# Where the FFN's moving operands begin in SBUF: one offset instead of fourteen

## The chip, the core and the metric

The kernel runs on one core of a Trainium2 chip. The metric is the device time of one execution in microseconds (us). TensorE (PE in the profile) multiplies matrices, VectorE (DVE), ScalarE (ACT) and GpSimd (POOL) work element by element, and SyncE (SP) issues the transfers. SBUF is the working memory: 128 partitions, each a run of bytes, in which every buffer has one byte address for all partitions. PSUM receives the results of the matrix multiplications.

A matmul has two operands in SBUF. The **stationary** operand, the weights, is loaded by an instruction of its own (LDWEIGHTS, engine PEld in the profile). The **moving** operand is then streamed past it, one column after another; a column is four bytes in each partition here. This text is about the byte address at which the moving operand begins, and speaks of it modulo 512 bytes: its *offset*.

## What is computed

```python
def _attn_ref(x, w_r, w_i, b_r, b_i):            # x: (8, 3008, 256)
    X = np.fft.rfft(x, axis=1)
    Yr = Xr @ w_r - Xi @ w_i + b_r
    Yi = Xr @ w_i + Xi @ w_r + b_i
    Yr = np.sign(Yr) * np.maximum(np.abs(Yr) - lam, 0.0)   # the same for Yi
    return np.fft.irfft(Yr + 1j * Yi, n=x.shape[1], axis=1)

def _moe_ref(x, w_in, w_out):                     # x: (24064, 256)
    h = x @ w_in                                  # (24064, 2048)
    g = h - np.tanh(h)
    return g @ w_out                              # (24064, 256)
```

The result of the first function, flattened to 24064 rows, is the input of the second, which the text calls the FFN.

## The kernel before

**The spectral part.** A sequence of 3008 is transformed as 64 times 47. Per batch, `Forward` does the transform over 47, `Spectrum` the one over 64, the linear layer, the shrinking and one half of the way back, and `Chunk.time` the other half. Between them the data goes through DRAM. This is a small share of the matmuls.

**The FFN.** Its 24064 rows are cut into 52 chunks: 50 of 470 columns (five groups of 94) and two of 282. A chunk goes through 16 steps, one for each 128 of the 2048 hidden columns, so there are 832 steps. A step has two halves:

- `up` (the matmuls of line 428): six matmuls into the PSUM buffer `h`. ScalarE then takes tanh (line 431), VectorE subtracts (line 433).
- `down` (line 449): six matmuls that add to the chunk's two results `o`, and that are finished at the 16th step.

Values are kept in two parts each, a rounded one and its remainder (`_h` and `_l`: `yh`, `yl` for the FFN's input, `gh`, `gl` for the hidden values, `win_h`, `win_l`, `wout_h`, `wout_l` for the weights), and three of the four products are made: hence six matmuls with 2 x 3 pairs. In `up` the moving operand is, in this order, `yh` part 0, `yh` part 1, `yh` part 0, `yh` part 1, `yl` part 0, `yl` part 1. In `down` it is `gh`, `gh`, `gl`, and again `gh`, `gh`, `gl`. With 470 columns there are 800 steps and so 9600 such matmuls; the other 384 have 282.

**The order of the work.** It is written out by hand. The main loop runs `up` two steps ahead of `down` (`AHEAD = 2`), and puts pieces of the spectral part between them from a table of slots. No scheduler moves anything.

**The buffers.** `yh` and `yl` have two buffers each, one for even and one for odd chunks; a buffer holds two parts of `PITCH` columns, of which 470 are used. `gh` and `gl` have three buffers each, used in turn, step after step. `PITCH` is 520, so the next part or buffer begins 2080 bytes further on. A pool places its buffers one behind the other, and the pools lie one behind the other in the order in which they are opened. `below`, a small constant for the shrinking of the first batch, lies in the first pool behind the FFN's weights; nearly everything else is behind it.

As the program is built, the FFN's weights begin at 128 modulo 512, and so does each slice of 128 columns of them, since such slices are 512 bytes long. The moving operands lie as follows:

| moving operand | offset of its buffers |
|---|---|
| `yh` part 0, part 1, even chunks | 256, 288 |
| `yl` part 0, part 1, even chunks | 384, 416 |
| `yh` part 0, part 1, odd chunks | 320, 352 |
| `yl` part 0, part 1, odd chunks | 448, 480 |
| `gh`, three buffers | 0, 32, 64 |
| `gl`, the buffers that go with them | 128, 160, 96 |

Of the kernel before, what the change touches and what calls it, by code (L numbers as in the profile page):

```python
# [10 lines left out]
F32 = mybir.dt.float32  # L11
# [55 lines left out]
def spectral_ffn(ctx, tc, x, w_r, w_i, b_r, b_i, w_in, w_out, f1, f2, i1, i2, out):  # L67
    nc = tc.nc
    P = 128
# [2 lines left out]
    CP = 5  # L72
    CT = CP * 94
    NF = FF // P
    PITCH = 520
    PSUM = bass.MemoryType.PSUM

    const = ctx.enter_context(tc.tile_pool(name="const", bufs=1))
# [314 lines left out]
    class Chunk:  # L393
# [14 lines left out]
        def time(self, t):  # L408
            n = self.n
            if t == 0:  # L410
                self.yh = work.tile([P, 2, PITCH], F32R, name="yh", tag="yh")
                self.yl = work.tile([P, 2, PITCH], F32R, name="yl", tag="yl")
            ps = ps_f.tile([P, 512], F32, name="ps_i2", tag="f")
# [8 lines left out]
        def up(self, f):  # L422
# [10 lines left out]
            nc.vector.tensor_tensor(out=g[:, :n], in0=h[:, :n], in1=th[:, :n], op=ALU.subtract)  # L433
            gh = ffn.tile([P, PITCH], F32R, name="gh", tag="g_h")
            nc.scalar.copy(out=gh[:, :n], in_=g[:, :n])  # L435
            gl = ffn.tile([P, PITCH], F32R, name="gl", tag="g_l")
            nc.vector.tensor_tensor(out=gl[:, :n], in0=g[:, :n], in1=gh[:, :n].bitcast(F32), op=ALU.subtract)  # L437
# [58 lines left out]
    with tc.manual_schedule(engines={E.PE, E.Activation, E.DVE, E.Pool, E.SP}):  # L496
# [6 lines left out]
        def keep_warm(n):  # L503
            for _ in range(n):
                nc.tensor.matmul(idle, warm[:, :P], warm, start=True, stop=True)

        keep_warm(8)
        below = const.tile([P, 32], F32, name="below")
        nc.vector.memset(below, -LAM)
        f1f = load_whole(f1, [P, P], "f1")  # L510
        first = [Forward(0, ch) for ch in range(NP // XC)]
# [169 lines left out]
```

## Time and profile before

| | us |
|---|---|
| time, median of 3 runs | 2746.91 (2746.25 to 2747.99) |
| time of the profiled execution | 2745.83 |
| its span, first to last instruction | 2744.1 |
| PE busy in it | 2707.5 |
| PEld busy | 2386.7 |
| VectorE busy | 1742.6 |
| ScalarE busy | 1375.6 |

In the profile, L428 is line 428 of the listing. A group's row gives its number of instructions, then busy us and the mean duration of one in ns, then the idle time of its engine just before them, with what ended it. The duration of a matmul there reaches past the start of the next one, because matmuls are pipelined: what a matmul costs is the time from its start to the start of the next one, and this text calls that its *interval*. The view by windows gives, for stretches that the reader chooses, each engine's busy time and its number of instructions; its last row is the sum over all stretches asked for, and the mean of one.

### The profile page before, as it was taken

Reading aid. Unit: us, or ns where it says so; the run is one execution under the profiler, and the core shown is the slowest. Engines: PE = TensorE matmul, PEld = TensorE weight load, DVE = VectorE, ACT = ScalarE, POOL = GpSimd, SP = SyncE. Lnnn points to the kernel's source line nnn. Section 1 sums busy time; section 2 is a strip of 40 time slices with the busy share of each in tenths; the row PEclk is TensorE's granted clock in tenths of the full one; section 3 lists DMA queues with packets and bytes.
Section 4 is the critical chain, followed back from the end, with each engine's and each line's share of the span. In section 5 each row is a group of like instructions: output and inputs, shape, how many; then the busy total and the mean of one; then the engine's idle time right before and its main releaser. Section 6 shows DMA issues by size and latency. Waiting matters only on the chain.

```text
span 2744.1 us, 36889 instructions
## 1 busy us (share of the span) xinstructions
PE 2707.5 (99%) x14114; PEld 2386.7 (87%) x14114; DVE 1742.6 (64%) x3059; ACT 1375.6 (50%) x2571; POOL 58.2 (2%) x47
## 2 busy tenths in 40 slices
PE   8799999999999999999999999999999999999999
PEld 5578888998889998898988998888988998888889
DVE  5796776667556666567655666656665666655555
ACT  3564455544554455545455444645455444444444
POOL 2130000000000000000000000000000000000000
PEclk9999999999999999999999999999999999999999
DMA  7432113111131113211023110311103111000000
GB/s 213 151 103 66 45 63 112 42 49 36 42 108 49 38 39 99 67 45 50 27 64 94 41 50 30 114 52 51 39 28 116 49 38 40 35 22 22 20 18 17
DMA packets 105217, 163.52 MB, mean 60 GB/s; under 512 B 7440, under 2 KB 71056, under 8 KB 104944
## 3 DMA queue, kind: packets, MB, share of 16 engines
q1 hardware_dynamic: 105040, 161.16, 18.8%
q8 instruction: 111, 1.82, 0.3%
q14 instruction: 66, 0.54, 0.1%
HBM read 86.16 MB, written 74.97 MB: 59 GB/s over the span
## 4 chain that ended last, share of the span: by engine, by line
PE 93%; DVE 4%; DMA 1%; ACT 1%; issue 1%; POOL 0%; SPq 0%; DVEq 0%; ACTq 0%; POOLq 0%
PE o L449 37%; PE h L428 37%; PE ps_v L297 4%; PE ps_i L415 4%; PE ps_f L277 3%; PE ps_t L297 2%; PE ps_f L225 1%; PE ps_f L227 1%; PE ps_f L226 1%; DVE y L322 1%; PE ps_i L332 1%; PE ps_i L333 1%; PE ps_i L334 1%; DMA a<-st 0%; DVE gl L437 0%
## 5 line engine op out<-in xcount | busy, mean ns | idle before, releaser
L433 DVE TENSOR_TENSOR g<-h,th 128x470 f32<-128x470 f32 (+1 forms) x832 | 531.9, 639 | 580.3 <-ACT th L431 576.8
L431 ACT ACTIVATE th<-h 128x470 f32<-128x470 f32 (+1 forms) x832 | 464.0, 558 | 792.4 <-PE h L428 791.1
L437 DVE TENSOR_TENSOR gl<-g,gh 128x470 fp32r<-128x470 f32 (+1 forms) x832 | 532.8, 640 | 289.3 <-ACT gh L435 220.5
L435 ACT CAST gh<-g 128x470 fp32r<-128x470 f32 (+1 forms) x832 | 484.1, 582 | 390.9 <-DVE g L433 380.9
L449 PE MATMUL o<-gh,wout_l 128*128 128x470 f32 (+1 forms) x1664 | 634.9, 382 | 1.2 <-ACT gh L435 1.2
L449 PE MATMUL o<-gl,wout_h 128*128 128x470 f32 (+1 forms) x1664 | 620.8, 373 | 3.4 <-DVE gl L437 3.3
L449 PE MATMUL o<-gh,wout_h 128*128 128x470 f32 (+1 forms) x1664 | 621.6, 374 | 0.0
L428 PE MATMUL h<-yh,win_l 128*128 128x470 f32 (+1 forms) x1664 | 487.8, 373 | 5.2 <-DVE g L433 4.7
L428 PE MATMUL h<-yh,win_h 128*128 128x470 f32 (+1 forms) x1664 | 485.6, 372 | 0.0
L428 PE MATMUL h<-yl,win_h 128*128 128x470 f32 (+1 forms) x1664 | 483.9, 372 | 0.0
L428 PEld LDWEIGHTS h<-yh,win_l 128*128 128x128 f32 x1664 | 312.2, 189 | 50.2 <-DVE g L433 6.6
L449 PEld LDWEIGHTS o<-gl,wout_h 128*128 128x128 f32 x1664 | 313.3, 188 | 47.8 <-DVE gl L437 7.1
L428 PEld LDWEIGHTS h<-yh,win_h 128*128 128x128 f32 x1664 | 310.8, 188 | 42.2
L449 PEld LDWEIGHTS o<-gh,wout_l 128*128 128x128 f32 x1664 | 313.7, 189 | 38.6 <-issue 1.6
L428 PEld LDWEIGHTS h<-yl,win_h 128*128 128x128 f32 x1664 | 311.6, 188 | 41.0
L449 PEld LDWEIGHTS o<-gh,wout_h 128*128 128x128 f32 x1664 | 313.7, 189 | 33.7
L322 DVE TENSOR_TENSOR y<-tb,ps_v 64x256 f32<-64x256 f32 x384 | 160.1, 417 | 10.5 <-ACT tb L369 6.5
L415 PEld LDWEIGHTS ps_i<-i,zin 96*128 96x128 f32 x1024 | 128.4, 194 | 5.0 <-issue 1.8
L415 PE MATMUL ps_i<-i,zin 96*128 96x94 f32 x1024 | 130.0, 275 | 1.1 <-DMA zin<-z 1.1
L277 PEld LDWEIGHTS ps_f<-f,at 128*128 128x128 f32 x768 | 101.2, 192 | 14.3 <-issue 9.0
L277 PE MATMUL ps_f<-f,at 128*128 128x128 f32 x768 | 102.9, 276 | 6.4 <-DMA at<-a 6.4
L92 DVE TENSOR_TENSOR x_l<-xt,x_h 94x512 fp32r<-94x512 f32 x112 | 78.6, 708 | 45.1 <-ACT x_h L91 45.1
(99 smaller groups left out, 2098.4 us busy)
## 6 DMA issues: line engine op xcount, KB each, us to landing
xt<-in_x SPq DMA_DIRECT2D x64, 384.0 KB, 3.7
at<-a SPq DMA_DIRECT2D x96, 256.0 KB, 2.8
z<-zo SPq DMA_DIRECT2D x96, 256.0 KB, 2.3
out<-ot SPq DMA_DIRECT2D x50, 470.0 KB, 3.0
a<-st SPq DMA_DIRECT2D x56, 384.0 KB, 3.1
zin<-z SPq DMA_DIRECT2D x42, 480.0 KB, 4.1
w_raw<-in_moe_w_in SPq DMA_DIRECT2D x8, 512.0 KB, 4.1
w_raw<-in_moe_w_out SPq DMA_DIRECT2D x8, 512.0 KB, 4.1
```

The lines of the kernel that those rows point to most:

```text
L92: rest.tensor_tensor(out=lo, in0=src, in1=hi.bitcast(F32), op=ALU.subtract)
L225: nc.tensor.matmul(pv, f1h, xl, start=True, stop=False)
L277: nc.tensor.matmul(pv[:, t, jj], self.at[:, jj, t * P:(t + 1) * P], rhs, start=True, stop=True)
L297: nc.tensor.matmul(dst, lhs[:, t], rhs[:, t, :], start=n == 0, stop=n == 5)
L322: nc.vector.tensor_tensor(out=y[ri * 64:(ri + 1) * 64, jj, :], in0=common(jj, ri), in1=self.vv[jj * 64:(jj + 1) * 64, ri * D:(ri + 1) * D] ...
L415: nc.tensor.matmul(ps[:, k * 94:(k + 1) * 94], self.zt[:, k, t * P:(t + 1) * P], i2t[:, p * 94:(p + 1) * 94], start=True, stop=True,)
L428: nc.tensor.matmul(h[:, :n], lhs[:, t, f * P:(f + 1) * P], rhs[:, t, :n], start=k == 0, stop=k == 5)
L431: nc.scalar.activation(out=th[:, :n], in_=h[:, :n], func=AF.Tanh)
L433: nc.vector.tensor_tensor(out=g[:, :n], in0=h[:, :n], in1=th[:, :n], op=ALU.subtract)
L435: nc.scalar.copy(out=gh[:, :n], in_=g[:, :n])
L437: nc.vector.tensor_tensor(out=gl[:, :n], in0=g[:, :n], in1=gh[:, :n].bitcast(F32), op=ALU.subtract)
L449: nc.tensor.matmul(self.o[t][:, :n], lhs[:, f, t * P:(t + 1) * P], rhs[:, :n], start=f == 0 and k == 0, stop=f == NF - 1 and k == 2,)
```

## The change

```diff
-    PITCH = 520
+    PITCH = 512
...
-        below = const.tile([P, 32], F32, name="below")
+        below = const.tile([P, P + 8], F32, name="below")
         nc.vector.memset(below, -LAM)
```

`PITCH` falls to 512 columns, so parts and buffers are 2048 bytes apart, and an offset no longer changes from one to the next. `below` grows from 32 to 136 columns, 416 bytes, which shifts what lies behind it. As the program is built, all fourteen moving operands of the table above now begin at 160 modulo 512. The weights of the FFN lie ahead of `below` and stay at 128. Most of the other buffers (`xt`, `zin`, `at`, the linear layer's weights, the temporary ones) go from 256 or 0 to 160 as well.

No instruction is added, removed or moved on any engine. The one row that differs is VectorE's, right at the start of the program, where it fills a constant of zeros, makes the tile `warm` of it, and fills `below`:

```order
 L498 MEMSET zero 128x512
 L500 CAST warm<-zero 128x512
-L509 MEMSET below 128x32
+L509 MEMSET below 128x136
 L241 COPY st<-ps_f_133 96x512
 L241 COPY st<-ps_f_143 96x512
```

The fill keeps its place and gets 104 more columns.

## The prediction

> **What bounds the kernel.** I read the page's busy times first, then the chain that ended last, then the groups of the two FFN lines with shapes kept apart, and then the waits of PE.
>
> ```profile
> PE 2707.5 (99%) x14114; PEld 2386.7 (87%) x14114; DVE 1742.6 (64%) x3059; ACT 1375.6 (50%) x2571; POOL 58.2 (2%) x47
> PE 93%; DVE 4%; DMA 1%; ACT 1%; issue 1%; POOL 0%; SPq 0%; DVEq 0%; ACTq 0%; POOLq 0%
> L449 PE MATMUL o<-gh,wout_l 128*128 128x470 f32 x1600 | 615.8, 385 | 1.2 <-ACT gh L435 1.2
> L449 PE MATMUL o<-gl,wout_h 128*128 128x470 f32 x1600 | 602.0, 376 | 3.4 <-DVE gl L437 3.3
> L428 PE MATMUL h<-yh,win_l 128*128 128x470 f32 x1600 | 474.2, 377 | 5.2 <-DVE g L433 4.7 <-ACT yh L419 0.3
> PE h L428 <- DVE g L433: 4.7, 4, 1.9
> PE o L449 <- DVE gl L437: 3.3, 7, 0.7
> ```
>
> PE is busy 99% of the span and is 93% of the chain. In the FFN it hardly waits: 4.7 and 3.3 us in all, in 4 and 7 cases, for the two operands that VectorE makes. So the time is the sum of the intervals of PE's matmuls, and the question is what one of the 9600 intervals of 470 columns is worth before and after. VectorE and ScalarE, at 64% and 50%, have room; whatever the new addresses do to them is behind PE.
>
> The mean duration in the group rows mixes all buffers and reaches over the next start, so I cut PE's time into halves of a step. Here is a stretch with nothing but FFN matmuls, in windows from one half's first matmul to the next half's first: `up`, `down` from the buffers at 0/128, `up`, `down` at 64/96, `up`, `down` at 32/160 (`gh`/`gl`). The columns are the window, its length, the busy time of PE, PEld, DVE, ACT and POOL with the number of their instructions, PE's granted clock, the DMA share and GB/s.
>
> ```profile
> 2375.54:2376.83 1.29, 1.29 (x8) 1.12 (x7) 0.68 (x2) 0.00 (x0) 0.00 (x0) 1.00 0.70 209
> 2376.83:2378.11 1.28, 1.28 (x8) 1.13 (x6) 0.43 (x1) 0.56 (x1) 0.00 (x0) 1.00 0.49 167
> 2378.11:2379.39 1.28, 1.28 (x8) 1.13 (x7) 0.63 (x2) 0.59 (x1) 0.00 (x0) 1.00 0.00 0
> 2379.39:2380.66 1.27, 1.27 (x8) 1.13 (x7) 0.66 (x2) 0.56 (x1) 0.00 (x0) 1.00 0.00 0
> 2380.66:2381.93 1.27, 1.27 (x7) 1.12 (x6) 0.62 (x2) 0.59 (x1) 0.00 (x0) 1.00 0.00 0
> 2381.93:2383.24 1.31, 1.31 (x7) 1.14 (x6) 0.71 (x2) 0.56 (x1) 0.00 (x0) 1.00 0.00 0
> ```
>
> Each window holds six matmuls (the counts include neighbours that reach in). PE has no idle time in any, the granted clock is 1.00 in all, and still six equal matmuls take 1.27 us in one and 1.31 in another. The buffers differ, and the spread, 3%, is many times what this measurement can tell from no change, about 0.2% or 5.5 us.
>
> **What an offset is worth.** I took all halves of this kind that run without a foreign matmul and without a stop (no interval of 240 ns or more), in one window each, and read the sum row; the first 190 of each kind, or all where there are fewer. In order: `down` at 0/128 (190), `down` at 32/160 (190), `down` at 64/96 (190), `up` of even chunks, 256 to 416 (138), `up` of odd chunks, 320 to 480 (144).
>
> ```profile
> sum 245.27, PE 245.27; mean PE 1.29
> sum 244.69, PE 244.69; mean PE 1.29
> sum 243.08, PE 243.08; mean PE 1.28
> sum 176.40, PE 176.40; mean PE 1.28
> sum 184.61, PE 184.61; mean PE 1.28
> ```
>
> Divided by six times the count, a mean interval is 215.2, 214.6 and 213.2 ns in `down`, and 213.0 and 213.7 in `up`. The three buffers are used equally, and so are the two chunk parities: the mean of `down` is 214.3, of `up` 213.4, of both **213.85 ns**.
>
> The trace has no matmul at 160 that follows one at 160, so the new interval must be taken from neighbours. I sorted single intervals by the offset of their own operand and of the next one, 190 windows each. In order: 32 then 32; 64 then 64; 0 then 0; 32 then 160; 160 then 32; 384 then 416; 0 then 128.
>
> ```profile
> sum 40.88, PE 40.88; mean PE 0.22
> sum 40.48, PE 40.48; mean PE 0.21
> sum 40.55, PE 40.55; mean PE 0.21
> sum 40.75, PE 40.75; mean PE 0.21
> sum 40.66, PE 40.66; mean PE 0.21
> sum 39.86, PE 39.86; mean PE 0.21
> sum 41.26, PE 41.26; mean PE 0.22
> ```
>
> That is 215.2, 213.1, 213.4, 214.5, 214.0, 209.8 and 217.2 ns. Three things are to be seen. The order of two offsets matters, up to 7 ns. Two equal offsets are nothing special: from 213.1 to 215.2. And of the equal ones, the pair at 32 is the slow one; 160 is 32 plus 128, and both lie 32 past a multiple of 64, while 0 and 64 do not.
>
> At this point a rule speaks against any effect. The Trainium skill, page "SBUF — State Buffer", section "Who interferes with whom", says that PE has two independent read ports, one for the moving operand and one for the weights, and never waits on anyone; the page "TensorE: Matmul & The Clock Gate", section "Back-to-back issue gap", gives N/2.4 + 2.5 ns, by which an estimate for 470 columns is 198.3 ns wherever the operand lies. By these the change is worth nothing. The rows above disagree twice: the mean is 213.85 ns, and buffers differ.
>
> **The change part by part.**
>
> *The FFN's operands, 9600 matmuls of 470 columns.* The nearest rows are those of the only buffers that hold an operand at 160, `down` at 32/160: 214.6 ns. There all six operands lie 32 past a multiple of 64, as all will after the change. Against 213.85 that is 0.79 ns more (from the unrounded 214.64), and 9600 x 0.79 = **+7.6 us**. Nearby bounds: the mean of 32-then-160 and 160-then-32, 214.2, gives +3.7 us; 32-then-32, 215.2, gives +12.6. Far bounds: 64-then-64 gives -7.7 us, 384-then-416 gives -39, 0-then-128 gives +32. I take the nearest row, and keep the far ones for the range.
>
> *The 384 matmuls of 282 columns.* At the same 0.79 ns they are 0.3 us.
>
> *The spectral part.* Its matmuls with large moving operands go from 256 to 160. The rows of three of its lines show their size:
>
> ```profile
> L297 PE MATMUL ps_v<-w_h,xh 128*128 128x256 f32 x336 | 67.6, 283 | 0.0
> L226 PE MATMUL ps_f<-x_h,f_l 94*96 94x512 f32 x112 | 44.7, 399 | 0.0
> L334 PE MATMUL ps_i<-z_h,i_h 128*128 128x512 f32 x84 | 33.1, 394 | 0.0
> ```
>
> Line 297 has 1512 such matmuls in six groups, lines 225 to 227 and 332 to 334 have 588. At most 283, 399 and 394 ns each, these are under 0.7 ms. No row shows them at another offset; if they move as the FFN's do, by 0 to 0.5% (+0.4% in the nearest row), it is 0 to 3 us, and as far below nothing by the pair at 64. These durations reach over the next start, so the true share is smaller; I take +1.
>
> *The fill of `below`.* It grows by 104 columns.
>
> ```profile
> 0.92 0.48 DVE L498 MEMSET zero<- 128x512 f32 x1 [0.92 <-PEq L660]
> 1.93 0.09 DVE L509 MEMSET below<- 128x32 f32 x1
> 7.43 0.69 DVE L241 COPY st<-ps_f 96x512 f32<-96x512 f32 x1 [5.42 <-PE ps_f L219]
> ```
>
> A fill of 512 columns takes 0.48 us and one of 32 takes 0.09, so 104 more are 104/480 of the 0.39 between them: 0.08 us. VectorE is then idle for 5.42 us, which covers it; without the cover it costs 0.08.
>
> *The element-wise work.* VectorE's and ScalarE's operands move as well. Should they get slower, the share of PE's waits above (8 us in all) is what they reach now, and they would have to fill the rest of their idle time before PE sees it. I count nothing.
>
> The sum is 7.6 + 0.3 + 1 = +8.9 us, on a profiled execution of 2745.8 us: 2754.7. That execution is 1.1 us below the median, so the forecast for the median is 2755.8, rounded to **2756 us**.
>
> **The rivals.**
>
> *No effect.* The offset only sorts the intervals by chance, because another thing that goes with the buffer sets them: the position in the half, or the weights. For it: 0-then-0 and 64-then-64 are within 0.8 ns of the mean. Against it: `down` has the same six positions and, over the steps, the same weights for each of its three buffers, and these differ by 1.9 ns. It gives 2747, and with the spectral part up to 3 us either way. The rules of the Trainium skill quoted above lead to this case.
>
> *Equal operands settle, and it becomes faster.* At the start, `keep_warm` (line 505) runs 18 matmuls of 512 columns with the same moving operand and the same weights. The windows hold its intervals 2 to 10 and the last 7:
>
> ```profile
> 21.32:23.41 2.09, 2.09 (x10) 1.69 (x9) 1.60 (x3) 0.00 (x0) 0.86 (x1) 1.00 0.72 176
> 23.41:25.00 1.59, 1.59 (x8) 1.31 (x7) 1.34 (x2) 0.44 (x1) 0.92 (x1) 1.00 1.02 319
> ```
>
> 2.09/9 is 232 ns, 1.59/7 is 227: the repeated matmul settled into a faster pace after ten, by 2.2%. With one offset for all operands the FFN has the same chance, in the stretches that nothing interrupts, two of which are these:
>
> ```profile
> 2374.47:2409.99 35.52, 35.52 (x168) 31.26 (x166) 18.43 (x30) 16.52 (x29) 0.00 (x0) 1.00 0.09 31
> 2417.79:2453.25 35.46, 35.46 (x167) 31.24 (x166) 18.42 (x30) 16.51 (x29) 0.00 (x0) 1.00 0.08 28
> ```
>
> 166 matmuls are many more than ten. A pace 2.2% below 213.85 is 209.1, near the fastest pair above, 209.8; it would bring -39 us if it held everywhere, 2708, and half of it if it held in half of the stretches, 2728. It decides if the sequence at 160 finds such a pace sooner than the spectral part interrupts it. Against it: 32-then-32, the only pair of its kind, is the slowest of the equal pairs, and the pace depends on the weights too, which are at 128, not at the operand's own offset as they were in `keep_warm`.
>
> *Equal operands lock badly, and it becomes much slower.* PEld is busy 87% of the span, so almost every matmul streams while the next weights are read, and all weights begin at 128. Today fourteen offsets average over good and bad relations to that. With one offset there is one relation, and if it is as bad as 0-then-128, at 217.2 ns, all 9600 pay 3.3 ns: +32 us, 2779. It decides if the relation of 160 to 128 is a bad one. Against it: intervals into and out of 160 are 214.5 and 214.0 today.
>
> **How the numbers follow.** The forecast, 2750 to 2761 by its nearby bounds, gets 0.46; of that about 0.13 lies under 2752.4, where it can't be told from no change. No effect gets 0.15, settling 0.20, locking 0.19. That is faster by over 0.2% 0.20, within it 0.28, slower 0.52. For the range I leave out the settled half below -24 us (about 0.10) and a little above the priced end of locking: 2723 to 2780.
>
> **What would show it.** In the profile after, the three groups of line 449 and the three of line 428 would come closer together, each near its slowest of before, and PE's waits would stay as they are. The halves at any buffer should take the same time, 1.288 us for six, that is 6 x 214.6 ns; 1.26 or less means that settling won, 1.30 or more that locking did. If the intervals still differ between the three `gh` buffers, offsets modulo 512 are not what counts. The forecast is wrong if 160 after 160 isn't like its neighbours at 32: no row of the trace has it.

## The result, and the profile after

| | before | after |
|---|---|---|
| median time, us | 2747.45 (4 runs) | 2722.26 (4 runs, 2717.52 to 2722.89) |
| span of the profiled execution, us | 2744.1 | 2720.4 |
| PE busy, us | 2707.5 | 2685.2 |

The change is a gain: the ratio of the times is 0.9909, with a 95% interval of 0.9896 to 0.9921, some 25 us. The forecast was 2756, a loss. One execution of e1 below took 9486.49 us and is left out of its ratio.

These are the lines of the page after that answer to those of before, and the rows of the same two FFN groups and of the same waits (views by groups with shapes apart, and by waits of PE).

```profile
PE 2685.2 (99%) x14114; PEld 2388.2 (88%) x14114; DVE 1741.2 (64%) x3059; ACT 1369.4 (50%) x2571; POOL 58.1 (2%) x47
PE 92%; DVE 5%; ACT 1%; DMA 1%; issue 1%; POOL 0%; SPq 0%; DVEq 0%; ACTq 0%; POOLq 0%
L449 PE MATMUL o<-gh,wout_l 128*128 128x470 f32 x1600 | 614.5, 384 | 0.8 <-ACT gh L435 0.8
L449 PE MATMUL o<-gl,wout_h 128*128 128x470 f32 x1600 | 598.3, 374 | 2.6 <-DVE gl L437 2.6
L428 PE MATMUL h<-yh,win_l 128*128 128x470 f32 x1600 | 469.1, 374 | 5.2 <-DVE g L433 4.7 <-ACT yh L419 0.3
PE h L428 <- DVE g L433: 4.7, 4, 1.9
PE o L449 <- DVE gl L437: 2.6, 6, 0.7
```

PE is busy 22.3 us less with the same 14114 matmuls, and it waits as little as before. Nothing went off the path; the matmuls themselves follow each other faster. The same sums as in the prediction, over 190 undisturbed halves of a step each, `down` first, then `up`, show by how much:

```profile
sum 241.12, PE 241.12; mean PE 1.27
sum 239.41, PE 239.41; mean PE 1.26
```

Per matmul that is 211.5 ns in `down` and 210.0 in `up`, where it was 214.3 and 213.4. The mean falls from 213.85 to 210.75, and 3.1 ns on 9600 matmuls are 30 us. The 25 measured are less, so what these sums leave out, the interrupted halves and the start, must gain less. In the first 200 us PE gets through fewer matmuls than before (674 for 689) and is busy longer: the granted clock was 0.91 there in this execution and 0.95 in the one before (last columns of the windows, before, then after):

```profile
0.00:200.00 200.00, 167.96 (x689) 123.25 (x690) 146.15 (x270) 101.22 (x188) 58.24 (x47) 0.95 0.51 156
```

```profile
0.00:200.00 200.00, 170.47 (x674) 125.56 (x675) 143.42 (x265) 98.10 (x182) 58.09 (x47) 0.91 0.52 154
```

What the faster pace looks like is seen in consecutive halves, `up`, `down`, `up`, `down`, in windows of the kernel after:

```profile
2401.01:2402.27 1.26, 1.26 (x7) 1.13 (x6) 0.70 (x2) 0.00 (x0) 0.00 (x0) 1.00 0.63 202
2402.27:2403.53 1.26, 1.26 (x7) 1.13 (x6) 0.41 (x1) 0.56 (x1) 0.00 (x0) 1.00 0.61 174
2403.53:2404.79 1.26, 1.26 (x7) 1.13 (x6) 0.61 (x2) 0.59 (x1) 0.00 (x0) 1.00 0.00 0
2404.79:2406.05 1.26, 1.26 (x7) 1.13 (x6) 0.69 (x2) 0.56 (x1) 0.00 (x0) 1.00 0.00 0
```

Where halves took 1.27 to 1.31 us before, each of these takes 1.26, whatever the transfers, VectorE and ScalarE do beside it. The sequence has settled. In the stretch of 166 matmuls that took 35.46 us before, the settled pace shows without any disturbance:

```profile
2399.96:2434.82 34.86, 34.86 (x167) 31.18 (x166) 18.36 (x30) 16.48 (x29) 0.00 (x0) 1.00 0.08 28
```

34.86/166 is 210.0 ns. A stretch of 166 intervals without a foreign matmul occurs nine times in every version; it is the yardstick of the experiments.

### The profile page after: what moved, and what is told of

The parts are those of the page before. It is cut to its first block, busy times and chain, and to the rows that moved or that the text cites. A ratio compares the mean times of both kernels' runs of the same rounds, so it can differ in the third digit from the quotient of the medians.

```text
span 2720.4 us, 36889 instructions
## 1 busy us (share of the span) xinstructions
PE 2685.2 (99%) x14114; PEld 2388.2 (88%) x14114; DVE 1741.2 (64%) x3059; ACT 1369.4 (50%) x2571; POOL 58.1 (2%) x47
## 4 chain that ended last, share of the span: by engine, by line
PE 92%; DVE 5%; ACT 1%; DMA 1%; issue 1%; POOL 0%; SPq 0%; DVEq 0%; ACTq 0%; POOLq 0%
PE o L449 36%; PE h L428 36%; PE ps_v L297 4%; PE ps_i L415 4%; PE ps_f L277 3%; PE ps_t L297 2%; PE ps_f L225 1%; DVE y L322 1%; PE ps_f L226 1%; PE ps_f L227 1%; PE ps_i L333 1%; PE ps_i L334 1%; PE ps_i L332 1%; DVE g L433 1%; DVE gl L437 0%
```

## The experiments

The *distance* below is the operand's offset less that of the FFN's weights, counted modulo 256: 32 in the kernel after (160 and 128). That 256 is the right number to count by is tested by f1. A ratio is to executions of the kernel before that were made along with the experiment's. Experiments that change only the common offset do it by the size of `below`, as the change does.

### Each part alone, and other common offsets

Two theories stood at the start. *Settling*: any common offset will do. *Place*: 160 is a good one.

**e1_at256**, the pitch alone.

```diff
-        below = const.tile([P, P + 8], F32, name="below")
+        below = const.tile([P, 32], F32, name="below")
```

> The pitch alone: all FFN moving operands at one offset, 256, buffers 2048 bytes apart; below as before. Settling (equal offsets let the sequence settle, whichever offset it is): a settled stretch at 210 ns per matmul as at 160, time near 2722 us, ratio near 0.991. Place (160 is a good place against the weights at 128, another common offset need not be): the settled interval is another one, anything from 206 to 220 ns, and the time differs from 2722 by up to 90 us.

Measured: ratio 1.0002 (0.9992 to 1.0012): no gain. The stretch of this kernel, and its sums for `down` and `up`, say why:

```profile
2420.44:2455.85 35.41, 35.41 (x167) 31.12 (x166) 18.41 (x30) 16.50 (x29) 0.00 (x0) 1.00 0.08 28
```

```profile
sum 243.96, PE 243.96; mean PE 1.28
sum 243.20, PE 243.20; mean PE 1.28
```

It settles, at 35.41/166 = 213.3 ns, and `up` runs at just that pace (243.20/1140). But 213.3 is hardly better than the 213.85 of the fourteen mixed offsets. Settling is there; it isn't the gain.

**e2_steps160**, the shift alone: the steps of 32 bytes stay, and begin at 160.

```diff
-    PITCH = 512
+    PITCH = 520
...
-        below = const.tile([P, P + 8], F32, name="below")
+        below = const.tile([P, 8], F32, name="below")
```

> The shift alone: the steps of 32 bytes of the kernel before are kept, but begin at 160 instead of 256 (yh 160, 192, 224, 256; yl 288 to 384; gh 416, 448, 480; gl 0, 32, 64); the spectral part lies at 160 as in the changed kernel. Settling and place both: no single offset, so no steady interval, mean near 213.8 ns, time within 8 us of 2747. If the gain came from the spectral part or the element-wise work having moved to 160: near 2722 instead.

Measured: ratio 0.9999 (0.9990 to 1.0008). The shift of everything else by itself brings nothing, and both parts of the change are needed. Its `down` from the buffers at 416/32, 448/64 and 480/0 (`gh`/`gl`):

```profile
sum 242.24, PE 242.24; mean PE 1.27
sum 242.57, PE 242.57; mean PE 1.28
sum 245.16, PE 245.16; mean PE 1.29
```

With mixed offsets the buffers differ again, 212.5, 212.8 and 215.1 ns.

**e3_at128** and **e4_at192**, a common offset equal to the weights', and 64 past it.

```diff
-        below = const.tile([P, P + 8], F32, name="below")
+        below = const.tile([P, 128], F32, name="below")      # e3; 144 in e4
```

> One common offset, 128, the same as the weights'. Settling: 210 ns, near 2722 us. Place: another interval; if reading the same place as the weights is what costs, the slowest of the common offsets, 217 ns or more, 2780 us or more.

> One common offset, 192, that is 64 past the weights' 128 and 32 past 160. Settling: 210 ns, near 2722 us. Place: another interval than at 160; nothing says which.

Measured: ratios 0.9995 (0.9985 to 1.0006) and 0.9988 (0.9977 to 0.9998). The second is 0.12% under before, where the change brought 0.9%. Both settle at 213.3 to 213.4 ns. The fear that reading at the weights' own offset would be the worst case was wrong. So *place* is right, and of four common offsets only 160 was good.

### The operand's own address, or its distance to the weights?

160 differs from 128, 192 and 256 in not being a multiple of 64, and in being 32 past the weights. Four kernels tell these apart.

**e5_at288** and **e6_at96**: other offsets that are 32 past a multiple of 64.

```diff
-        below = const.tile([P, P + 8], F32, name="below")
+        below = const.tile([P, 40], F32, name="below")       # e5; 120 in e6
```

> One common offset, 288: 32 past a multiple of 64, 160 past the weights' 128. Own address (the settled pace goes by the operand's place in 64 bytes: 210 ns at 32, 213.3 at 0): 210 ns, near 2720 us. Distance in 64 (it goes by the distance to the weights modulo 64): 210 ns too. Exact distance (only 32 past the weights, modulo 256 or 512, is good): 213.3 ns, near 2745 us.

> One common offset, 96: 32 past a multiple of 64, 32 ahead of the weights' 128. Own address and distance in 64: 210 ns, near 2720 us. Exact distance: 213.3 ns, near 2745 us.

**e7_w160_o192** and **e8_w160_o160**: 32 bytes are put ahead of the weights, which then begin at 160.

```diff
+    pad = const.tile([P, 8], F32, name="pad")
     win_h = const.tile([P, 2, FF], F32R, name="win_h")
...
-        below = const.tile([P, P + 8], F32, name="below")
+        below = const.tile([P, 136], F32, name="below")      # e7; 128 in e8
```

> Weights and operands both 32 bytes further on: weights at 160, operands at 192, the distance of 32 kept, the operand at a multiple of 64. Own address: 213.3 ns, near 2745 us. Distance in 64 and exact distance: 210 ns, near 2720 us.

> The operands stay at 160, the weights go from 128 to 160: distance 0. Own address, or the place 160 alone: 210 ns, near 2720 us. Distance in 64 and exact distance: 213.3 ns, near 2745 us.

Measured: e5 1.0012 (1.0000 to 1.0023), e6 1.0003 (0.9992 to 1.0015), e7 **0.9920** (0.9891 to 0.9949; two executions), e8 0.9994 (0.9983 to 1.0006). The stretch in e5, in e7 and in e8:

```profile
2419.86:2455.28 35.41, 35.41 (x167) 31.12 (x166) 18.40 (x30) 16.50 (x29) 0.00 (x0) 1.00 0.09 28
```

```profile
2400.08:2434.94 34.86, 34.86 (x167) 31.18 (x166) 18.36 (x30) 16.48 (x29) 0.00 (x0) 1.00 0.09 28
```

```profile
2414.11:2449.53 35.42, 35.42 (x167) 31.13 (x166) 18.40 (x30) 16.49 (x29) 0.00 (x0) 1.00 0.08 28
```

In e5 the operands lie 32 past a multiple of 64, as in the change, and gain nothing. In e7 they lie at 192, where e4 gained nothing, and the gain is back, since the weights moved along. In e8 they lie at 160, as in the change, and the gain is gone, since the weights came closer. The distance decides, not the address.

### How far the distance repeats, and how narrow it is

**f1_at416** has distance 288; **f4_at224** has 96; **g1_at64** has 192, the last of the eight steps of 32 in 256 bytes.

```diff
-        below = const.tile([P, P + 8], F32, name="below")
+        below = const.tile([P, 72], F32, name="below")       # f1; 152 in f4, 112 in g1
```

> One common offset, 416: distance 288 from the weights' 128, which is 32 modulo 256. If the distance counts modulo 256 (or less): settles at 210 ns, near 2722 us. If it counts modulo 512: 213.3 ns, near 2745 us.

> One common offset, 224: distance 96. If 32 is the only good step of 32: 213.3 ns, 2745 us. If good places return every 64 bytes but not at distance 160 and 224 (which both gave 213.3): 210 ns; this is thought unlikely.

> One common offset, 64: distance -64, that is 192 modulo 256, the last of the eight steps of 32. If 32 is the only good one: settles at 213.3 ns, near 2744 us. If not: 210 ns, near 2721 us.

Measured: f1 **0.9904** (0.9876 to 0.9933; two executions), f4 0.9997 (0.9986 to 1.0009), g1 **1.0086** (1.0057 to 1.0115; two executions). The stretch in f1:

```profile
2396.68:2431.54 34.86, 34.86 (x167) 31.18 (x166) 18.36 (x30) 16.50 (x29) 0.00 (x0) 1.00 0.09 28
```

Distance 288 is as good as 32, so, by this one pair, the distance counts modulo 256. It doesn't count modulo 128 or 64: then 160 (e5) would be as good as 32, and it isn't. And 192 is a bad place: 2769.97 us against 2746.32. A line of g1's page, and its stretch:

```profile
PE 2735.3 (99%) x14114; PEld 2401.0 (87%) x14114; DVE 1743.1 (63%) x3059; ACT 1375.1 (50%) x2571; POOL 58.1 (2%) x47
```

```profile
2483.50:2519.47 35.97, 35.97 (x167) 31.43 (x166) 18.45 (x30) 16.51 (x29) 0.00 (x0) 1.00 0.09 28
```

It settles too, at 35.97/166 = 216.7 ns, and PE's busy time is 28 us above that of before. The expectation had only 210 and 213.3 in it.

**f2_d16**, **f3_d48**, **g2_d24** and **g3_d40** go between the steps of 32: the operands begin some columns into their buffers.

```diff
+    SH = 4                                               # f2, f3; 6 in g2, 2 in g3
...
-                    nc.tensor.matmul(h[:, :n], lhs[:, t, f * P:(f + 1) * P], rhs[:, t, :n], start=k == 0, stop=k == 5)
+                    nc.tensor.matmul(h[:, :n], lhs[:, t, f * P:(f + 1) * P], rhs[:, t, SH:SH + n], start=k == 0, stop=k == 5)
...                                                       # the same at gh, gl and where they are written
-        below = const.tile([P, P + 8], F32, name="below")
+        below = const.tile([P, 128], F32, name="below")      # f2, g2; 136 in f3, g3
```

> All four operands begin 4 columns into buffers at 128: offset 144, distance 16. If the good distances are a stretch that ends above 0 and includes 32: 210 ns and near 2722 us, or better, down to 206.7; if 32 is the lower edge of it: 213.3 ns, 2745 us.

> All four operands begin 4 columns into buffers at 160: offset 176, distance 48. If the good stretch goes on above 32: 210 ns or better, 2722 us or less; if 32 is its upper edge: 213.3 ns, 2745 us (distance 64 gave that).

> All four operands begin 6 columns into buffers at 128: distance 24. Narrow (only 32 settles at 210): 213.3 ns or the mixture of distance 16, 2738 to 2745 us. Wide (a stretch of distances round 32): 210 ns, near 2721 us, or a better pace, 206.7 ns, near 2690 us.

> All four operands begin 2 columns into buffers at 160: distance 40. Narrow: 213.3 ns, 2738 to 2745 us. Wide: 210 ns, near 2721 us, or a better pace, 206.7 ns, near 2690 us.

Measured: f2 0.9982 (0.9971 to 0.9993), f3 0.9972 (0.9961 to 0.9983), g2 0.9990 (0.9979 to 1.0001), g3 0.9984 (0.9973 to 0.9995). None has the change's gain; the most, 0.3%, is f3's. So 32 is narrow: 8 bytes to either side the pace of 210 is gone. The stretch in g3:

```profile
2412.74:2448.15 35.41, 35.41 (x167) 31.29 (x166) 18.40 (x30) 16.50 (x29) 0.00 (x0) 1.00 0.09 28
```

In g3 every buffer lies where the change has it, and only the FFN's operands begin 8 bytes further on. So it is where the operands begin that counts, and not where the other buffers lie.

Two stretches of f2:

```profile
706.79:741.83 35.04, 35.04 (x167) 31.23 (x166) 18.31 (x30) 16.54 (x29) 0.00 (x0) 1.00 0.10 31
2451.36:2487.33 35.97, 35.97 (x167) 31.29 (x166) 18.47 (x30) 16.48 (x29) 0.00 (x0) 1.00 0.08 28
```

f2 has two paces. Of its nine stretches of this length the first three run at 211.1 ns (35.04 over 166) and the other six at the bad pace, 216.7 (35.97 over 166). This is how it can be no slower than before as a whole. Here the sequence has more than one way to settle; what chooses between them isn't shown.

All paces, from two such stretches of each kernel, and for f2 from all nine:

| distance modulo 256 | kernels | 166 intervals, us | settled pace, ns |
|---|---|---|---|
| 32 | after, e7, f1 | 34.86 | 210.0 |
| 0, 64, 96, 128, 160, 224 | e3 and e8, e4, f4, e1, e5, e6 | 35.41 to 35.42 | 213.3 to 213.4 |
| 24, 40, 48 | g2, g3, f3 | 35.41 to 35.42 | 213.3 to 213.4 |
| 192 | g1 | 35.95 to 35.97 | 216.6 to 216.7 |
| 16 | f2 | 35.04 or 35.97 | 211.1 or 216.7 |

In each of these kernels other than f2 the nine stretches agree to 0.02 us.

### Does each half settle by itself?

**g4_mixed** keeps `yh` and `yl` at 160 and puts `gh` and `gl` at 192.

```diff
+    cvt.tile([P, 8], F32, name="pad", bufs=1)
     ffn = ctx.enter_context(tc.tile_pool(name="ffn", bufs=3))
```

> yh and yl stay at 160 (distance 32), gh and gl go to 192 (distance 64), all buffers 2048 bytes apart. Each by itself: up settles near 210 ns as soon as a few of its six matmuls have run, down near 213.3; half the gain, near 2733 us. Only the whole loop: neither settles within six matmuls, mean 213 to 214 ns, near 2744 us.

Measured: ratio 0.9969 (0.9953 to 0.9985), about a third of the gain. The sums of `down` and `up`, and the stretch:

```profile
sum 244.14, PE 244.14; mean PE 1.28
sum 240.87, PE 240.87; mean PE 1.27
```

```profile
2409.03:2444.35 35.32, 35.32 (x167) 31.31 (x166) 18.41 (x30) 16.50 (x29) 0.00 (x0) 1.00 0.09 28
```

`up` takes 211.3 ns, close to its 210.0; `down` takes 214.2, slower than at 192 throughout (213.3 settled in e4). If each half simply had its own settled pace, the stretch would run at the mean of 210.0 and 213.3, which is 211.7; it runs at 212.8 (35.32 over 166). That fits halves that go by their own distance and lose a little at each change from one distance to the other, but the loss itself wasn't isolated.

## Why the prediction was wrong

**What bounds the kernel** was right: PE's intervals and nothing else. PE's waits hardly moved, and the time followed the pace of 470-column matmuls in every kernel run here.

**That an offset has a price** was right, and *no effect* is refuted: with the same instructions, medians from 2719 us (f1) to 2770 (g1) came out by addresses alone. The rule of the Trainium skill that was weighed there (page "SBUF — State Buffer", section "Who interferes with whom": two independent read ports, and PE waits on no one) doesn't describe this kernel: moving the weights by 32 bytes under the same operands (e8) took the whole gain away (35.42 us for 34.86 in the stretch).

**The step that failed** is "I take the nearest row": 214.6 ns from the halves at 32/160, hence +7.6 us. The runs give -3.1 ns in undisturbed halves instead. That row was wrong in two ways. Its operands are at distances 160 and 32 by turns, and the sorting that likened them, by what is left over 64, has nothing to it: e5, at the distance 160, gains nothing. And intervals in a mixed sequence are those of a sequence that never settles, so no row of before shows the pace of a settled one at a given distance; 32-then-32 took 215.2 ns at distance 160, and settled (e5) the same distance takes 213.3. In the trace of before, one pair hinted at the answer: 384-then-416, at 209.8, the fastest of the pairs shown there, goes from distance 0 to 32. I had it as a far bound.

**The rival *settling*** had the right sign and nearly the right pace, 209.1 ns for the measured 210.0, but not the right condition. It looked to the one offset alone, and e1, e3, e4, e5, e6, e8 and f4 settle at theirs without a gain. That 209.1 came so near is luck: the 2.2% were taken from `keep_warm`, whose operand and weights begin at the same address, and at that distance, 0, the FFN settles at 213.3 to 213.4 (e3, e8). The price put on it, 39 us, belongs to 209.8; by 209.1 it would have been some 45. My second argument against it, that the pace depends on the weights too, was the key, used for the wrong side.

**The rival *locking badly*** was right in its mechanism too, one relation to the weights for all matmuls. It exists at distance 192, with 216.7 ns and 2770 us, where it was priced at 217.2 and 2779. That price is near by luck too: it was that of 0-then-128, which goes from distance 128 to 0, and both of these settle at 213.3 to 213.4 (e1, e3). Which of the two rivals comes true is decided by the distance, and the trace of before couldn't say it for 32. That was put as a doubt at the end, but the range stopped at 2723, because only half of the settled case was let into it, and the forecast was made as though the doubt were small.

**The small terms.** The spectral part was to cost 1 us for its move to 160. The three rows for it after (groups with shapes apart) read 67.3, 44.9 and 33.2 us where they read 67.6, 44.7 and 33.1: it is nothing. (The forecast's nearby bounds, 2750 and 2761, aren't made alike: with the small terms the lower one is 2752.)

```profile
L297 PE MATMUL ps_v<-w_h,xh 128*128 128x256 f32 x336 | 67.3, 282 | 0.0
L226 PE MATMUL ps_f<-x_h,f_l 94*96 94x512 f32 x112 | 44.9, 401 | 0.0
L334 PE MATMUL ps_i<-z_h,i_h 128*128 128x512 f32 x84 | 33.2, 395 | 0.0
```

The fill of `below` and the element-wise work were rightly counted at nothing.

What stays open is why. The runs show that the distance between the moving operand and the weights counts. That the reading of the next weights beside the stream couples the two would fit, but it isn't shown: no run took the weight loads away. A version better than the change wasn't found: e7 and f1 equal it within their intervals.

## What to carry to other kernels

Where PE is the bound and equal matmuls follow each other at unequal intervals, look at the addresses: give all moving operands of the hot loop one distance to the weights, and try that distance in steps of 32 bytes over 256, since it was worth from -1.0% (f1) to +0.9% (g1) here and one common offset alone was worth nothing (e1). All this is for one width, 470 columns of four bytes; no other was looked at. An interval from a mixed sequence isn't the price of the same operand in a uniform one; where a sequence can settle, measure it settled. And an edit that shifts the operands against the weights, such as another size of a small constant that lies between them, can move the time of a kernel like this by a per cent or more: the change and g1 differ in nothing else, and take 2722 and 2770 us.

## What was not expected of the hardware

At eleven of the twelve distances the settled pace is one of three values, 210.0, 213.3 and 216.7 ns, to about 0.1 ns, in equal steps of 3.33 ns. The twelfth (f2, distance 16) ran in two ways in the same execution, and one of them, 211.1 ns, is none of the three. The distance counts modulo 256 bytes (f1 against e5), but 8 bytes beside the good one are enough to lose it (g2, g3). And `keep_warm`, quoted in the prediction with its pace falling from 232 to 227 ns, was a true picture of settling, though not of the gain: after ten intervals it stays at one pace.
